# A last token tile computed in three column pieces, and a table of shifts in the order in which an attention and feed-forward kernel is recorded

## The chip, the cores and the metric

The kernel runs on one core of one Trainium2 chip. The core has a matrix engine (TensorE, PE in the profile, with its weight loads as PEld), a vector engine (VectorE, DVE), a scalar engine (ScalarE, ACT), a general engine (GpSimd, POOL) and a synchronisation engine (SyncE, SP), whose queue issues nearly all DMAs here. Every engine executes its own list of instructions in order; semaphores tie the lists together. The metric is the device time of one execution in microseconds.

## The reference

The input x has 2,048 tokens of 640 features. Two rounds run over it, with the same weights; each adds an attention with a memory and then a feed-forward network to x. In code cut to what matters:

```
x = x + A(layernorm(x))      # attention with memory
x = x + B(layernorm(x))      # relu(x @ w1) @ w2, 640 -> 1728 -> 640
x = x + A(layernorm(x))
x = x + B(layernorm(x))

A: q, k, v = x @ wq, x @ wk, x @ wv; 32 heads of 20; 4 segments of 512 tokens
   for each segment s:
     a_dot = softmax(q k^T / sqrt(20), causal inside the segment) v
     a_mem = phi(q) M / (phi(q) z)         # phi(t) = t + 1 if t > 0 else exp(t)
     o = g * a_mem + (1 - g) * a_dot       # g = sigmoid(beta), per head
     M, z = M + phi(k)^T v, z + sum(phi(k))
   return o @ wo
```

## The kernel before

All weights and all of x stay in the core's fast memory. Work is cut by round (0 or 1, called a or b) and segment (0 to 3, s), written (round, segment) below, and inside a segment by token tiles of 128 (four, NJ) and by groups of four heads (eight, G).

For one segment of attention: layer norm of four token tiles (`lnorm`, L705: statistics at L679 and L681, a small POOL power at L695, the normalised tokens at L725, then a transposing DMA issued by SP through `turn`, L701). Projections to q and k (`proj_part`, groups of five matmuls at L658 or L661, evacuated by ACT or DVE at L857/L858) and to v (`proj_v`, evacuated at L912). q and k go to a scratch tensor in HBM (`spill`, L946) and come back with four heads on separate partition groups (`fill`, L993, tile `pad`). Scores run as bursts of matmuls at L1177 into two PSUM slots, ACT takes their exponential (L1239) and POOL applies the causal mask (L1251). `apply` multiplies by v (L1271), `turn_pair` transposes the result back by DMA on SP (tile `otk` from `otu`), `divide` (L1357 to L1365) normalises it into `o_sb`, `mem_read` (L1057 to L1072) and `combine` (L1384) add the memory part, `turn_o` transposes `o_sb` on SP, and `out_proj` multiplies by wo and adds to x (L1393). Then the layer norm for the feed-forward network (`ln_b`), the network itself (`ffn` and `ffn_rest`, evacuated at L1475/L1476) and the addition to x through `add_half` (L1393). In round 1, `store` writes each token tile to the output (L1519).

A group of matmuls has two forms: whole (L658, 128 weight columns) and in quarters (L661, four matmuls of 32 weight columns that run beside each other). Scores use a third form, in which the rows are split. Whichever form is in force is kept where a group has both.

The order of all this is not written by hand. Each kind of work is a Python generator, a stream, that yields one step at a time: an operation, a need for an event, a slot of a buffer, or a spawned stream. `Sched.run` (L286) looks at the next step of every stream, works out from its own table of durations when the step could start, and records the step with the smallest key: start plus a lateness, then priority, then rank, then stream number (L319). Recording appends the step to its engine's list, and each engine on the chip then executes its list in that order. Whatever is recorded later sees the times and slots that the earlier choices left.

Streams are numbered in the order of `S.add` (L1541 to L1577), spawned ones after them:

```
 0 scores      1 exps        2 causal      3 apply       4 free_v
 5 turn_pair   6 divide      7 turn_o      8 out_proj(0) 9 out_proj(1)
10 ln_b(0)    11 ln_b(1)    12 fill       13 spill      14 combine
15 phi_(0)    16 phi_(1)    17 mem_read(0) 18 mem_read(1) 19 turn_k
20 mem_write  21 first_sums 22-25 first_one(0..3)       26 first_ln_b
27 proj_ln    28 proj_first 29 proj_one(0) 30 proj_one(1) 31 proj_v
32 ffn        33 ffn_rest   34 store      35 warm_pe    36 consts
37 loads      38 late_loads 39, 40, 41 ... spawned (the first ones by proj_first)
```

A stream made with `each` (L1525) goes through the eight (round, segment) pairs and has rank 4 x round + segment; the others have rank 0, and a spawned stream has the rank of its parent. `proj_ln` is the layer norm before attention, `ln_b(0)` and `ln_b(1)` are the first and the last two token tiles of the one before the feed-forward network.

For the second feed-forward product (L1502 to L1511) each of the four token tiles is made as two groups of 320 output columns, of 14 accumulating steps each; each group has a PSUM bank, and its addition to x is spawned as a stream. The store of a tile waits for both halves.

Of the kernel before, what the change touches and what calls it, by code (L numbers as in the profile page):

```python
# [7 lines left out]
ALU = mybir.AluOpType  # L8
# [5 lines left out]
NSEG = 4  # L14
# [5 lines left out]
NJ = L // 128  # L20
# [141 lines left out]
        self.gen = gen  # L162


LONE_NS = 300.0
SWITCH_NS = 96.0
COLS_LAG = 1500.0
# [9 lines left out]
class Sched:  # L177


    def __init__(self, prog):  # L180
        self.P = prog
        self.free = {e: 800.0 for e in ENGS}
        self.t = {}
        self.events = {}
        self.streams = []
        self.dma_free = 0.0
        self.rank = {}
        self.mode = "full"
        self.landed = set()

    def add(self, prio, gen):
        self.streams.append([prio, gen, None, None, False])
        self.rank[id(gen)] = 0

    def at(self, tk):
# [90 lines left out]
    def run(self):  # L286
        while True:
            best = None
            moved = True
            while moved:  # L290
                moved = False
                for st in list(self.streams):
                    had, ended = st[2], st[4]
                    self._settle(st)
                    moved = moved or st[4] != ended
                    moved = moved or st[2] is not had
            heads = []
            for n, st in enumerate(self.streams):
                if st[4]:
                    continue  # L300
                if isinstance(st[2], Op):
                    heads.append((st[0], n, st, self._alts(st[2]), st[2], self._late(st[2])))
                elif isinstance(st[2], Either):
                    both, lone = st[2].fn()
                    if both is not None:
                        heads.append((st[0], n, st, self._alts(both), both, 0.0))
                    if lone is not None:
                        heads.append((8, n, st, self._alts(lone), lone, LONE_NS))
            for prio, n, st, alts, op, late in heads:
                ok = []  # L310
                for end, start, k, e in alts:
                    if not any(p2 < min(prio, HOLDERS) and st2 is not st
                               and any(e2 == e and s2 + HOLD_TOL[e] < end for _, s2, _, e2 in al2[:1])
                               for p2, _, st2, al2, _, _ in heads):
                        ok.append((end, start, k))
                if not ok:
                    continue
                end, start, k = min(ok)
                key = (round(start + late), 0.5 if op.urgent else prio, self.rank[id(st[1])], n)  # L319
                if best is None or key < best[0]:  # L320
                    best = (key, st, end, start, k, op)
            if best is None:
                stuck = [st for st in self.streams if not st[4]]
                if not stuck:
                    return
                raise RuntimeError("stuck: " + "; ".join(
                    str(getattr(st[2], "key", None) or [s.name for s in getattr(st[2], "slots", [])][:2]) for st in stuck))
            _, st, end, start, k, op = best
            e, hold, fns, tail = op.alts[k]
            if e == "pe":  # L330
                op.mode = self._mode(op)
                self.mode = op.mode
                if op.mode == "cols" and op.cols is not None:
                    fns = op.cols
            waits, slot = op.waits, None
            for s in op.take:
                s.free = False
            if op.acq is not None:
                slot = self._pick(op.acq)
                slot.free = False  # L340
                waits = waits + slot.tks
                fns = [(lambda eng, fn=fn, slot=slot: fn(eng, slot), mark) for fn, mark in fns]
            self.P.waits(e, waits)
            self.free[e] = end
            if op.dma is not None:
                tk = self.P.dma(e, fns[0][0], op.dma)
                self.landed.add((id(tk[0]), tk[1]))
                self.dma_free = max(self.dma_free, start + 300.0) + tail[1]
                self.t[(id(tk[0]), tk[1])] = max(self.dma_free, end) + tail[0]
                if tail[2]:  # L350
                    self.free[e] = max(end, self.dma_free)
                out = tk
            else:
                marks = []
                for fn, mark in fns:
                    tk = self.P.op(e, fn, mark)
                    if tk is not None:
                        self.t[(id(tk[0]), tk[1])] = end + tail
                        marks.append(tk)
                out = marks[0] if len(marks) == 1 else (marks or None)  # L360
            st[2], st[3] = None, ((slot, out) if slot is not None else out,)
# [52 lines left out]
def bass_interleave_layers__memory_aug_infini_attn__dense_activation_relu__prompt_kernel(  # L414
    nc, A_x, A_wq, A_wk, A_wv, A_wo, A_beta, B_x, B_w1, B_w2, out,
):
    with contextlib.ExitStack() as es:
# [3 lines left out]
        S = Sched(P)  # L421
# [21 lines left out]
        x_sb = sb("x_sb", [128, TT, D])  # L443
# [25 lines left out]
        MISC = [Slot(ps[:, 4 + k, :], "misc%d" % k) for k in range(4)]  # L469
# [922 lines left out]
        def add_half(t, hf, bk, tk, waits=()):  # L1392
            ta = yield dve(320, 1, lambda e: e.tensor_tensor(  # L1393
                x_sb[:, t, 320 * hf:320 * hf + 320], x_sb[:, t, 320 * hf:320 * hf + 320], bk.ap[:, 0:320], ALU.add),
                [tk] + list(waits), urgent=True)
            bk.release(ta)
            return ta
# [67 lines left out]
        def ffn(b, s):  # L1465
            xtk = yield Need("hx", b, s)
            xt, xtk = xtk[0], xtk[1:]
            yield Acq([HT])
            S.set("hT", b, s)
            w1t = yield Need("w10")  # L1470
            hr = [("hr", b, s, dc) for dc in range(NFULL)]
            tk = None

            def square(dc, bk, tk):
                th = yield evac(512, 1, lambda e: e.tensor_scalar(hT[:, dc, :], bk.ap[:, :], 0.0, None, ALU.max),  # L1475
                                lambda e: e.activation(hT[:, dc, :], bk.ap[:, :], ACT.Relu), [tk] + HT.tks)  # L1476
                bk.release(th)
                S.set("hr", b, s, dc, tks=[th])

            for dc in range(NFULL):  # L1480
                if dc >= 2:
                    yield Need(*hr[dc - 2])
                if 128 * (dc + 1) > DFF // 2 >= 128 * dc:
                    w1t = yield Need("w11")
                bk, tk = yield from group(MISC, L, [
                    (w1_r[:, k, dc * 128:(dc + 1) * 128], feat(xt, k)) for k in range(FC)], xtk + w1t)
                yield Spawn(6, square(dc, bk, tk))
            HALF[b, s, 0] = tk
            if (b, s) in HALF:
                xt.release(tk, HALF[b, s])  # L1490
            w2t = yield Need("w2")
            hrest = yield Need("hR", b, s)
            sums = [[] for _ in range(NJ)]

            def residual(i, hf, bk, tk):
                ta = yield from add_half(4 * s + i, hf, bk, tk)
                S.set("sum", b, s, 2 * i + hf)
                sums[i].append(ta)
                if len(sums[i]) == 2:
                    S.set("xB", b, s, i, tks=sums[i])  # L1500

            for i in range(NJ):  # L1502
                for hf in range(2):
                    cs = slice(hf * 320, (hf + 1) * 320)
                    if 2 * i + hf >= 2:
                        yield Need("sum", b, s, 2 * i + hf - 2)
                    bk, tk = yield from group(MISC, 320, [
                        (hT[:, dc, i * 128:(i + 1) * 128], w2_r[:, dc, cs], Need(*hr[dc])) for dc in range(NFULL)] + [
                        (hR[:, (i % 2) * 128:(i % 2) * 128 + 128], w2_r[:, NFULL + i // 2, cs], hrest)], w2t)
                    yield Spawn(6, residual(i, hf, bk, tk))  # L1510
            HT.release(tk)  # L1511

        def store(b, s):
            if b == 0:
                return
            for i in range(NJ):
                t = 4 * s + i
                tks = yield Need("xB", b, s, i)
                S.last = yield dma("sp", dout, 163840, lambda e, t=t: e.dma_start(  # L1519
                    out[0, t * 128:(t + 1) * 128, :], x_sb[:, t, :]), tks)  # L1520
# [90 lines left out]
```

## Time and profile before

| | us |
|---|---|
| median of 4 executions | 558.92 (557.24 to 560.11) |
| the profiled execution, its own time | 559.04 |
| its span, first to last instruction | 557.3 |
| PE busy | 546.0 |
| DVE busy | 415.6 |
| ACT busy | 405.6 |
| POOL busy | 191.6 |
| last matmul ends | 554.53 |

How to read it: busy is the time in which an engine executed an instruction, and matmuls overlap each other in a pipeline, so PE can be busy without being at its peak. Lines of a timeline give start, duration, engine, source line, operation, what is written and read, shape and count; in square brackets stands the idle time of the engine before it and what ended it. A list of waits gives engine, line and tile that waited, what it waited for, the total, the number of times and the longest. In a table of stretches each engine has its busy time and, in brackets, its instructions; PEclk is the granted clock of the matrix engine as a share of full speed, and the last two columns are the DMA engines' busy share and rate. SPq is SP's queue, which issues DMAs.

### The profile page before, as it was taken

Reading aid. Unit: us, or ns where it says so; the run is one execution under the profiler, and the core shown is the slowest. Engines: PE = TensorE matmul, PEld = TensorE weight load, DVE = VectorE, ACT = ScalarE, POOL = GpSimd, SP = SyncE. Lnnn points to the kernel's source line nnn. Section 1 sums busy time; section 2 is a strip of 40 time slices with the busy share of each in tenths; the row PEclk is TensorE's granted clock in tenths of the full one; section 3 lists DMA queues with packets and bytes.
Section 4 is the critical chain, followed back from the end, with each engine's and each line's share of the span. In section 5 each row is a group of like instructions: output and inputs, shape, how many; then the busy total and the mean of one; then the engine's idle time right before and its main releaser. Section 6 shows DMA issues by size and latency. Waiting matters only on the chain.

```text
span 557.3 us, 18813 instructions
## 1 busy us (share of the span) xinstructions
PE 546.0 (98%) x8209; PEld 307.5 (55%) x8209; DVE 415.6 (75%) x1062; ACT 405.6 (73%) x514; POOL 191.6 (34%) x302
## 2 busy tenths in 40 slices
PE   8998999999999999999999999999999999999998
PEld 7554554456454555646456554565555654666756
DVE  5967889888898898897778988889965767335102
ACT  5699889899667887797788887887765787432140
POOL 5346345333443344343433443335410433201000
PEclk9999999999999999999999999999999999999999
DMA  8696999844574158274284423772426512344101
GB/s 271 145 226 159 216 193 218 226 61 91 101 159 85 27 105 180 50 111 83 58 196 91 91 45 112 154 125 21 67 59 167 106 45 30 86 88 60 41 2 49
DMA packets 130003, 61.30 MB, mean 110 GB/s; under 512 B 108802, under 2 KB 119810, under 8 KB 129922
## 3 DMA queue, kind: packets, MB, share of 16 engines
q1 hardware_dynamic: 129504, 59.62, 49.7%
q8 instruction: 64, 1.05, 0.8%
q10 hardware_dynamic: 418, 0.49, 0.3%
q14 instruction: 17, 0.14, 0.1%
HBM read 20.57 MB, written 12.85 MB: 60 GB/s over the span
## 4 chain that ended last, share of the span: by engine, by line
PE 81%; DVE 7%; DMA 7%; ACT 2%; SPq 1%; issue 1%; POOL 0%; ACTq 0%; POOLq 0%
PE ps L658 38%; PE ps L661 24%; PE ps L1177 8%; PE ps L1271 6%; DMA otk<-otu 3%; ACT PT L1239 2%; PE ps L1057 1%; DMA pad<-scr 1%; PE ps L1114 1%; PE ps L635 1%; DMA xnT<-xn_tok 1%; PE ps L1451 1%; DMA phk<-phs 1%; DVE o_sb L1365 1%; PE ps L1310 1%; DVE xn_tok L725 1%
## 5 line engine op out<-in xcount | busy, mean ns | idle before, releaser
L1239 ACT ACTIVATE PT<-ps 128x1024 bf16<-128x1024 f32 x320 | 309.1, 1027 | 65.9 <-PE ps L1177 61.6
L1251 POOL TENSOR_SCALAR_AFFINE_SELECT PT<-PT 128x512 bf16<-128x512 bf16 x256 | 165.9, 666 | 267.7 <-ACT PT L1239 267.6
L1393 DVE TENSOR_TENSOR x_sb<-x_sb,ps 128x320 bf16<-128x320 bf16 x128 | 60.5, 479 | 69.2 <-PE ps L661 55.5
L658 PE MATMUL ps<-w_r,hT 128*128 128x320 bf16 x508 | 81.5, 300 | 0.0
L661 PE MATMUL ps<-xnT,w_r 128*32 128x512 bf16 x1144 | 68.3, 379 | 0.0
L1177 PE MATMUL ps<-pad 20*128 20x512 bf16 (+3 forms) x1024 | 63.4, 301 | 3.1 <-ACT PT L1239 2.0
L658 PEld LDWEIGHTS ps<-w_r,hT 128*128 128x128 bf16 x508 | 47.4, 98 | 23.7 <-issue 5.2
L658 PE MATMUL ps<-xnT,w_r 128*128 128x512 bf16 x234 | 57.7, 380 | 0.7 <-DMA xnT<-xn_tok 0.7
L679 DVE BATCH_NORM_STATS2 stats<-x_sb 128x6 f32<-128x320 bf16 x124 | 55.6, 471 | 3.1 <-DMA x_sb<-in_A_x_dram 2.7
L1476 ACT ACTIVATE hT<-ps 128x512 bf16<-128x512 f32 x57 | 34.1, 599 | 22.7 <-PE ps L661 20.8
L661 PE MATMUL ps<-w_r,hT 128*32 128x320 bf16 x1296 | 49.6, 299 | 0.0
L1177 PEld LDWEIGHTS ps<-pad 20*128 20x128 bf16 x1024 | 17.9, 92 | 54.8 <-issue 24.6
L1281 DVE CAST otu<-ps 128x512 bf16<-128x512 f32 x51 | 34.9, 684 | 11.6 <-PE ps L1271 11.4
L661 PEld LDWEIGHTS ps<-xnT,w_r 128*32 128x32 bf16 x1144 | 29.5, 97 | 24.3
L1271 PE MATMUL ps<-PT,v_aug 128*21 128x128 bf16 (+3 forms) x896 | 40.5, 301 | 0.0
L661 PEld LDWEIGHTS ps<-w_r,hT 128*32 128x32 bf16 x1296 | 34.2, 97 | 9.2
L1475 DVE TENSOR_SCALAR hT<-ps 128x512 bf16<-128x512 f32 x47 | 32.2, 685 | 6.8 <-PE ps L658 5.3
L658 PE MATMUL ps<-wo_r,oT 128*128 128x320 bf16 x223 | 35.4, 300 | 0.4 <-DVE x_sb L1393 0.4
L695 POOL TENSOR_TENSOR rstd<-lnU,mhalf 128x2 f32<-128x2 f32 (+2 forms) x26 | 20.6, 791 | 44.3 <-DVE lnU L691 42.1
L658 PEld LDWEIGHTS ps<-xnT,w_r 128*128 128x128 bf16 x234 | 20.9, 97 | 24.5 <-issue 5.3
L1022 ACT ACTIVATE stg<-stg 128x512 bf16<-128x512 bf16 x50 | 31.5, 634 | 2.5 <-DVE rtmp L1020 2.2
L857 DVE CAST stg<-ps 128x512 bf16<-128x512 f32 x43 | 29.2, 683 | 5.2 <-PE ps L658 4.8
(108 smaller groups left out, 707.9 us busy)
## 6 DMA issues: line engine op xcount, KB each, us to landing
pad<-scr SPq DMA_DIRECT2D x124, 80.0 KB
scr<-stg SPq DMA_DIRECT2D x34, 256.0 KB, 3.3
out_dram<-x_sb SPq DMA_DIRECT2D x16, 160.0 KB, 1.8
w_r<-in_B_w_dram SPq DMA_DIRECT2D x10, 216.0 KB, 2.6
w_r<-in_B_w_dram SPq DMA_DIRECT2D x13, 160.0 KB, 2.9
x_sb<-in_A_x_dram SPq DMA_DIRECT2D x10, 160.0 KB, 3.3
scr<-w_r SPq DMA_DIRECT2D x5, 256.0 KB, 2.7
wv_r<-in_A_wv_dram SPq DMA_DIRECT2D x1, 800.0 KB, 8.9
```

The lines of the kernel that those rows point to most:

```text
L658: return e.matmul(view(dst.ap, b), a, b, start=(k == 0), stop=(k == last))
L661: return e.matmul(view(dst.ap[rows], b), part, b, start=(k == 0), stop=(k == last))
L679: tk = yield dve(320, 1, lambda e, c2=c2: e.bn_stats(stats6[:, t % 12, c2, :], x_sb[:, t, c2 * 320:(c2 + 1) * 320]), xt)
L1022: te = yield act(512, lambda e, q=q: e.activation(q, q, ACT.Exp), [tr] + p, psum=False)
L1177: fns.append([(lambda e, z=z, j=j, hh=hh, N=N, o=o, sl=sl, q=hh % 2: e.matmul(slot.ap[:, q, o:o + N], sl.ap[32 * hh:32 * hh + DH, z, 0, 12 ...
L1239: tx = yield act(1024, lambda e, dst=dst, src=src: e.activation(dst, src, ACT.Exp, scale=SCALE), sc + pw)
L1251: tm = yield pool(600.0, lambda e, reg=reg: e.affine_select(out=reg, in_=reg, pattern=[[0, 4], [1, 128]], compare_op=ALU.is_ge, fill=0.0, ...
L1271: fns.append((lambda e, OD, j=j, hh=hh: e.matmul(OD.ap[32 * hh:32 * hh + DH + 1, 128 * j:L], VAUG[vx(a, s)][:, j, 4 * g + hh, :], pt.ap[:, ...
L1281: te = yield evac(L, 1, lambda e: e.tensor_copy(dst, OD.ap), lambda e: e.activation(dst, OD.ap, ACT.Copy), [tk] + OTU[0].tks)
L1393: ta = yield dve(320, 1, lambda e: e.tensor_tensor(x_sb[:, t, 320 * hf:320 * hf + 320], x_sb[:, t, 320 * hf:320 * hf + 320], bk.ap[:, 0:32 ...
L1475: th = yield evac(512, 1, lambda e: e.tensor_scalar(hT[:, dc, :], bk.ap[:, :], 0.0, None, ALU.max), lambda e: e.activation(hT[:, dc, :], b ...
L1476: lambda e: e.activation(hT[:, dc, :], bk.ap[:, :], ACT.Relu), [tk] + HT.tks)
```

## The change

It has three parts. In the last token tile of the last segment of round 1, the second group of 320 columns is made as two groups of 160, each with its own addition to x; the store of that tile becomes three stores of 320, 160 and 160 columns, each after its own addition. A table NUDGE, with thirteen entries (stream number, rank), adds a number of nanoseconds to the first part of the key of that stream's steps while it has that rank; it shifts the place in the order, not the start that the planner reckons with. And streams that have ended are dropped from the planner's list, with the stream number now kept in the stream itself, so that numbers stay the same.

```diff
--- before.py
+++ after.py
@@ -162,6 +162,21 @@
         self.gen = gen
 
 
+NUDGE = {
+    (5, 0): -100,
+    (8, 2): -100,
+    (11, 0): -900,
+    (14, 0): 200,
+    (18, 0): 900,
+    (24, 2): 200,
+    (27, 3): 100,
+    (27, 6): 450,
+    (34, 3): -450,
+    (35, 3): 200,
+    (38, 4): 450,
+    (39, 4): 450,
+    (41, 0): 450,
+}
 LONE_NS = 300.0
 SWITCH_NS = 96.0
 COLS_LAG = 1500.0
@@ -183,13 +198,15 @@
         self.t = {}
         self.events = {}
         self.streams = []
+        self.count = 0
         self.dma_free = 0.0
         self.rank = {}
         self.mode = "full"
         self.landed = set()
 
     def add(self, prio, gen):
-        self.streams.append([prio, gen, None, None, False])
+        self.streams.append([prio, gen, None, None, False, self.count])
+        self.count += 1
         self.rank[id(gen)] = 0
 
     def at(self, tk):
@@ -286,6 +303,7 @@
     def run(self):
         while True:
             best = None
+            self.streams = [st for st in self.streams if not st[4]]
             moved = True
             while moved:
                 moved = False
@@ -295,7 +313,8 @@
                     moved = moved or st[4] != ended
                     moved = moved or st[2] is not had
             heads = []
-            for n, st in enumerate(self.streams):
+            for st in self.streams:
+                n = st[5]
                 if st[4]:
                     continue
                 if isinstance(st[2], Op):
@@ -316,7 +335,7 @@
                 if not ok:
                     continue
                 end, start, k = min(ok)
-                key = (round(start + late), 0.5 if op.urgent else prio, self.rank[id(st[1])], n)
+                key = (round(start + late + NUDGE.get((n, self.rank[id(st[1])]), 0)), 0.5 if op.urgent else prio, self.rank[id(st[1])], n)
                 if best is None or key < best[0]:
                     best = (key, st, end, start, k, op)
             if best is None:
@@ -1492,22 +1511,26 @@
             hrest = yield Need("hR", b, s)
             sums = [[] for _ in range(NJ)]
 
-            def residual(i, hf, bk, tk):
-                ta = yield from add_half(4 * s + i, hf, bk, tk)
-                S.set("sum", b, s, 2 * i + hf)
+            def residual(i, hf, bk, tk, c0, n):
+                t = 4 * s + i
+                ta = yield dve(n, 1, lambda e: e.tensor_tensor(
+                    x_sb[:, t, c0:c0 + n], x_sb[:, t, c0:c0 + n], bk.ap[:, 0:n], ALU.add), [tk], urgent=True)
+                bk.release(ta)
+                S.set("sum", b, s, 2 * i + hf, tks=[ta])
                 sums[i].append(ta)
                 if len(sums[i]) == 2:
                     S.set("xB", b, s, i, tks=sums[i])
 
             for i in range(NJ):
-                for hf in range(2):
-                    cs = slice(hf * 320, (hf + 1) * 320)
+                last = (b, s, i) == (1, NSEG - 1, NJ - 1)
+                for hf, c0, n in ((0, 0, 320), (1, 320, 160), (2, 480, 160)) if last else ((0, 0, 320), (1, 320, 320)):
+                    cs = slice(c0, c0 + n)
                     if 2 * i + hf >= 2:
                         yield Need("sum", b, s, 2 * i + hf - 2)
-                    bk, tk = yield from group(MISC, 320, [
+                    bk, tk = yield from group(MISC, n, [
                         (hT[:, dc, i * 128:(i + 1) * 128], w2_r[:, dc, cs], Need(*hr[dc])) for dc in range(NFULL)] + [
                         (hR[:, (i % 2) * 128:(i % 2) * 128 + 128], w2_r[:, NFULL + i // 2, cs], hrest)], w2t)
-                    yield Spawn(6, residual(i, hf, bk, tk))
+                    yield Spawn(6, residual(i, hf, bk, tk, c0, n))
             HT.release(tk)
 
         def store(b, s):
@@ -1515,6 +1538,12 @@
                 return
             for i in range(NJ):
                 t = 4 * s + i
+                if (s, i) == (NSEG - 1, NJ - 1):
+                    for hf, c0, n in ((0, 0, 320), (1, 320, 160), (2, 480, 160)):
+                        tks = yield Need("sum", b, s, 2 * i + hf)
+                        S.last = yield dma("sp", dout, 256 * n, lambda e, c0=c0, n=n: e.dma_start(
+                            out[0, t * 128:(t + 1) * 128, c0:c0 + n], x_sb[:, t, c0:c0 + n]), tks)
+                    return
                 tks = yield Need("xB", b, s, i)
                 S.last = yield dma("sp", dout, 163840, lambda e, t=t: e.dma_start(
                     out[0, t * 128:(t + 1) * 128, :], x_sb[:, t, :]), tks)
```

## The prediction

> **What bounds the kernel now.** I read the busy table of the page first, then the busy time by stretch, then what the matmul engine waited for, and last the timeline of the end.
>
> ```profile
> PE 546.0 (98%) x8209; PEld 307.5 (55%) x8209; DVE 415.6 (75%) x1062; ACT 405.6 (73%) x514; POOL 191.6 (34%) x302
> PE 81%; DVE 7%; DMA 7%; ACT 2%; SPq 1%; issue 1%; POOL 0%; ACTq 0%; POOLq 0%
> ```
>
> PE is busy for 98% of the span and carries 81% of the chain that ended last. Next, eight stretches; the first two numbers are the length and PE's busy time in it.
>
> ```profile
> 0.00:20.00 20.00, 17.74 (x156) 13.65 (x157) 12.82 (x38) 10.12 (x23) 7.34 (x23) 1.00 0.67 204
> 20.00:110.00 90.00, 87.36 (x1189) 45.24 (x1190) 75.95 (x208) 82.15 (x104) 40.18 (x61) 1.00 0.88 209
> 110.00:160.00 50.00, 49.42 (x631) 27.50 (x623) 43.68 (x108) 41.46 (x51) 19.34 (x30) 1.00 0.51 100
> 160.00:240.00 80.00, 78.68 (x1092) 41.80 (x1094) 70.49 (x186) 63.49 (x75) 32.07 (x49) 1.00 0.44 91
> 240.00:350.00 110.00, 109.96 (x1490) 58.27 (x1490) 91.45 (x222) 91.52 (x113) 46.31 (x69) 1.00 0.49 101
> 350.00:430.00 80.00, 78.29 (x1205) 43.68 (x1194) 63.66 (x162) 59.71 (x79) 24.11 (x36) 1.00 0.50 96
> 430.00:484.00 54.00, 54.00 (x720) 30.28 (x719) 37.35 (x93) 40.22 (x46) 20.72 (x33) 1.00 0.35 73
> ```
>
> PE's idle time, length less busy, is 2.64 + 0.58 + 1.32 + 0.04 + 1.71 + 0.00 = 6.29 us from 20 to 484 us. That is nearly all a better order can win: the work itself is not changed, and from 484 us on PE has only feed-forward matmuls left and runs through to 554.5. The granted clock is 1.00 throughout. A burst of scores (L1177) between other matmuls also costs a change of array form, which this table counts as busy: in the records a gap of about 108 ns lies on either side of a burst. The number of bursts stays; two bursts placed together would save two gaps, 0.2 us. What PE waited for:
>
> ```profile
> PE ps L1177 <- ACT PT L1239: 2.0, 4, 0.7
> PE ps L635 <- POOL mhalf L585: 1.6, 1, 1.6
> PE ps L1177 <- DMA pad<-scr: 1.0, 2, 0.8
> PE ps L658 <- DVE w_r L857: 0.9, 1, 0.9
> PE ps L658 <- DMA xnT<-xn_tok: 0.7, 1, 0.7
> ```
>
> Each is a single case of at most 0.9 us (the 1.6 is the start): places where the recorded order reached something that came late. There is no one large stall to remove.
>
> **The last tile.** The end of the timeline, and the store line's landing:
>
> ```profile
> 552.32 0.31 PE L661 MATMUL ps<-w_r,hR 128*32 128x320 bf16 x4
> 552.46 1.94 PE L661 MATMUL ps<-w_r,hT 128*32 128x320 bf16 x52
> 554.22 0.31 PE L661 MATMUL ps<-w_r,hR 128*32 128x320 bf16 x4
> 554.58 0.49 DVE L1393 TENSOR_TENSOR x_sb<-x_sb,ps 128x320 bf16<-128x320 bf16 x1 [1.42 <-PE ps L661]
> ...
> DMA to landing us min/median/max: 1.8/1.8/4.1
> ...
> 395.91 0.34 PE L1057 MATMUL ps<-BD,phs 128*32 128x147 bf16 x12
> 396.09 1.04 PE L661 MATMUL ps<-xnT,w_r 128*32 128x512 bf16 x16
> ```
>
> After the last matmul (554.53) come a 0.49 us add, the issue at 555.10, 1.79 us to landing and 0.4 us to the end.
>
> PE: a 320-column group takes 554.22 - 552.32 = 1.90 us for 56 quarter matmuls. Its second half becomes two groups of 160. The nearest narrow row is memory reading in the same form: 12 matmuls of 147 columns start within 396.09 - 395.91 = 0.18 us, 15 ns each, so 56 of 160 take 56 x 15 x 160/147 = 0.92 us, and two groups 1.84 to 1.90 us. I take +0.0. From the other side, a matmul of 160 columns that took as long as one of 320 would make the extra group cost a full 1.90 us; the 147 row is so near that I keep only +0.3 as the bad end.
>
> A rule speaks against the halving here. "TensorE: Matmul & The Clock Gate", section "LDWEIGHTS (loading the stationary operand)", has a load cost its columns divided by 1.2 in ns, whatever the rows; 32 columns are then 27 ns, and by it, as an estimate, two groups of 56 loads would take 3.0 us instead of 1.90, which would turn this part into a loss of 1.1 us. The row with a load and a matmul every 15 ns contradicts that for quarter loads.
>
> DVE: the last add falls from 320 to 160 columns. An add of 128x320 takes 489 ns there; a two-input operation on 128x160 (L626) takes 316 ns. That is -0.17 us on the path. The extra add (316 ns) lies beside PE's last group.
>
> SP and DMA: one store becomes three. The first two leave beside the remaining matmuls, the second about 0.9 us before the third, and an issue holds SP for 0.33 us, so the third finds SP free. Of the 1.79 us from issue to landing, the packets take 0.61 us (128 of 1,280 bytes, 55 ns each, by the DMA records); 256-byte packets take 18 ns and 512-byte ones 27, so 320-byte ones should take about 21 and the burst 0.25 us: -0.3 us, at best -0.5, and at worst +0.2 if writes this short cost extra. Together: 0.0 - 0.17 - 0.3 = **-0.47 us**, between -0.7 and +0.5.
>
> **The table.** Keys are (stream number, rank). Streams are numbered in the order of the S.add calls, and only those made by `each` or spawned from one carry a rank above 0. So (24,2), a first_one, (35,3) warm_pe, (38,4) late_loads and (39,4), the first spawned, never have that rank; (14,0) combine and (18,0) mem_read issue nothing in segment 0; (34,3) store returns at once for b = 0. Seven entries of thirteen do nothing. The six others:
>
> - (41,0), +450: evacuation of the third projection group, on ACT at 10.80 us. ACT had been idle 1.14 us before it and no other work stands on ACT or PE in these microseconds, so recording it later changes no queue: 0.0, at worst 0.45 us, which is its whole shift.
> - (27,3), +100, and (27,6), +450: layer norm before attention for segments (0,3) and (1,2). Each is 17 DVE instructions, one POOL power and two SP transposes, of which DVE has 8 statistics at 471 ns and 4 normalisations at 521 ns. They let other DVE work by. The tokens are wanted some 100 and 40 us later (scores of (0,3) start near 181 us, of (1,2) near 351), so nothing behind waits. What can pay is DVE's other work: PE waited 0.4 us in all between 57 and 92 us, and nothing between 286 and 312. Gain 0 to 0.4.
> - (11,0), -900: second half of the layer norm before feed-forward of segment (0,0): 9 DVE instructions, one POOL power (0.80 us), one transpose on SP. They now stand from 78.36 to 88 us with gaps filled by casts and memory work. Recorded up to 0.9 us early they wait at the head of DVE's queue: for the residual adds, and for the power before the normalisation. Queued behind are casts (683 ns each) that free PSUM banks for PE. DVE is busy 32.00 of 35 us there, so it has 3.0 us to give. In return feed-forward (first at 91.19 us) can start earlier and fill PE. Between -0.4, the stretch's waits, and +0.9, one hold that passes through; I take 0.
> - (8,2), -100: out projection, left half, of segment (0,2): 20 matmuls and 4 adds from 195.6 on. A ready matmul (135 ns) goes ahead of a burst of scores. The nearest wait is 0.6 us, of scores on exps at 195.30. Between -0.6 and +0.3 (two matmuls ahead of a burst, ACT waiting); I take -0.2.
> - (5,0), -100: all 28 otk transposes on SP, 1.2 to 1.5 us each on the queue. Mostly the steps that they overtake belong to other engines, so SP's order stays: 0, unless a pad fill falls behind one (below).
>
> The direct sum, with half of the 0.4 for the norms, is -0.2 - 0.2 = -0.4 us. Beyond it, any change of order changes the planner's later choices, and the waits listed are dealt anew. Their squares (0.6, 0.7 and 0.2 on exps, 0.8 and 0.2 on pads, 0.9, 0.7, 0.4 and smaller) sum to about 3.6, so one deal scatters by 1.9 us and two against each other by 2.7: an estimate that takes the waits as independent. It favours no side.
>
> **Sum.** The profiled execution took 559.04 us: span 557.3 and 1.7 around it, 0.1 above the median 558.92. 559.04 - 0.47 - 0.4 = 558.2, and 558.1 against the median.
>
> **Rivals.**
> 1. The table finds an order without most of the waits. For it: 2.64 of the 6.29 us lie between 20 and 110 us, where three of the moved steps are. Against: 240 to 350 us, where the largest late shift sits, has 0.04 us to win. With 2.4 to 5 us of the 6.29 gone: 559.0 - 0.5 - 3.5 = 555.
> 2. Slower: at the end of segment (1,2) a pad fill leaves later. SP's queue there, and the wait that it already causes:
>
> ```profile
> 415.34 1.42 SPq L946 DMA_DIRECT2D scr<-stg  x2
> 418.25 2.91 SPq L701 DMA_TRANSPOSE oT<-o_sb  x2
> 421.26 1.73 SPq L993 DMA_DIRECT2D pad<-scr  x4
> 423.04 1.32 SPq L946 DMA_DIRECT2D scr<-stg  x3
> ...
> 426.15 0.40 PE L1177 MATMUL ps<-pad 20*128 20x512 bf16 x4 [0.84 <-DMA pad<-scr]
> ```
>
> PE has used up its other work at 425.3 and idles 0.84 us until the pads land, so there is no margin: each microsecond that a step ahead on SP is late is one of PE. One more pair of transposes ahead (2.91), or a wait at SP's head like that of this fill for the scratch (3.3), gives 559.0 - 0.5 + 3.3 = 561.8. It decides from 2.8 us of delay on.
> 3. The live entries change nothing of weight, and only the last tile tells: 558.5.
>
> **How the numbers follow.** Half a percent, 2.8 us, is about what a measurement of this kernel can tell from no change. Small gain with the waits about as many as before: 0.34; nothing but the tile: 0.06; both are within it. Rival 1: 0.34; rival 2 and other new stalls: 0.26. The likeliest time is 558.1; its own range is 556.2 to 561.6. Reaching into rival 1 (to 554, which wants 5 us of waits gone; 1 in 12 below) and rival 2 (to 562.6; 1 in 9 above) makes 554.0 to 562.6.
>
> **What would show it.** The last add 128x160 at about 0.32 us, three store issues, the last landing near 1.5 us; 128x160 groups that end within 0.1 us of today's pace. PE's idle time from 20 to 484 us between 4 and 8.5 us. Layer norm steps of (0,0) earlier than 84 to 88 us. Wrong if a PE wait over 2 us appears, if the number of changes of array form moves by more than ten (1.1 us), or if the idle falls under 4 us.

## The result and the profile after

The changed kernel takes 557.52 us where the kernel before takes 559.21, both medians: a ratio of 0.9967, 95% interval 0.9958 to 0.9976, or by that ratio 1.85 us less. The forecast was 558.1 against 558.92, 0.8 us less, with a range of 554.0 to 562.6 and "within half a percent" as the likeliest outcome. The direction and that outcome came true; the size is a little over twice the forecast, and it came from the table, the tile adding nothing that the runs can tell. The profiled execution took 557.63 us, 0.1 above its median, with a span of 555.8.

The busy table and the chain of the changed kernel (its lines are 19 further down than before for most of the program; the last additions to x are at L1516, the stores at L1544 and L1548):

```profile
PE 545.4 (98%) x8259; PEld 307.4 (55%) x8259; DVE 416.5 (75%) x1067; ACT 404.0 (73%) x510; POOL 192.6 (35%) x302
PE 85%; DVE 7%; DMA 5%; SPq 1%; ACT 1%; issue 1%; POOL 0%
```

The bound is the same engine. The stretches, length and PE's busy time first:

```profile
20.00:110.00 90.00, 85.68 (x1121) 44.48 (x1119) 73.94 (x202) 81.60 (x104) 40.31 (x61) 1.00 0.90 203
110.00:160.00 50.00, 49.84 (x732) 27.55 (x731) 45.40 (x111) 41.14 (x50) 19.36 (x30) 1.00 0.52 112
160.00:240.00 80.00, 79.82 (x1104) 43.15 (x1106) 69.98 (x185) 63.11 (x73) 32.24 (x49) 1.00 0.44 89
240.00:350.00 110.00, 109.74 (x1416) 57.78 (x1417) 90.41 (x221) 88.77 (x112) 42.59 (x65) 1.00 0.49 96
350.00:430.00 80.00, 79.92 (x1230) 44.52 (x1229) 64.97 (x167) 62.84 (x81) 27.42 (x41) 1.00 0.53 102
```

PE's idle from 20 to 484 us is 4.32 + 0.16 + 0.18 + 0.26 + 0.08 + 0.00 = 5.00 us, 1.29 less than before. It fell by 2.97 us between 110 and 430 and rose by 1.68 before 110. The last matmul ends at 552.77 in place of 554.53. The largest waits of PE:

```profile
PE ps L677 <- DVE om_sb L1091: 1.3, 1, 1.3
PE ps L1196 <- DMA pad<-scr: 1.0, 1, 1.0
PE ps L677 <- DVE w_r L876: 0.9, 1, 0.9
PE ps L1196 <- ACT PT L1258: 0.8, 2, 0.6
```

The first is new: at 107.5 us a feed-forward group waits for a PSUM bank that memory reading frees through DVE (L1091). The waits for x_sb, for the DMA transposes of xnT and for two of the exponentials are gone; one profiled execution each can't say which of these are gone for good, since single waits move from execution to execution (last section).

The end of the changed kernel, and how its three stores (L1544) land:

```profile
551.56 0.24 PE L680 MATMUL ps<-w_r,hR 128*32 128x160 bf16 x4
551.63 1.07 PE L680 MATMUL ps<-w_r,hT 128*32 128x160 bf16 x52
552.53 0.24 PE L680 MATMUL ps<-w_r,hR 128*32 128x160 bf16 x4
552.83 0.32 DVE L1516 TENSOR_TENSOR x_sb<-x_sb,ps 128x160 bf16<-128x160 bf16 x1 [0.65 <-PE ps L680]
...
L1544 SPq DMA_DIRECT2D out_dram<-x_sb x3: 332/332/1055, 551.4 to 553.2; - x3
DMA to landing us min/median/max: 2.1/2.2/2.9
...
q8 instruction: 65, 1.06, 0.8%
```

A group of 160 columns takes 552.53 - 551.56 = 0.97 us and the add 0.32 us, as forecast. But the third issue holds SP for 1.055 us in place of 0.33, and the landings take 2.1 to 2.9 us where 1.5 was forecast. From the last matmul to the end are 3.04 us, against 2.76 before. The last line counts 16 KB packets of instructions: 65, before 64. The 65th runs from 552.46 to 553.86 us, while all three stores are in flight (issued at 551.40, 552.21 and 553.17, landed at 553.52, 555.12 and 555.40).

### The profile page after: what moved, and what is told of

Its sections match the earlier page's. It is cut to its first block, busy times and chain, and to the rows that moved or that the text cites. A ratio compares the mean times of both kernels' runs of the same rounds, so it can differ in the third digit from the quotient of the medians.

```text
span 555.8 us, 18919 instructions
## 1 busy us (share of the span) xinstructions
PE 545.4 (98%) x8259; PEld 307.4 (55%) x8259; DVE 416.5 (75%) x1067; ACT 404.0 (73%) x510; POOL 192.6 (35%) x302
## 3 DMA queue, kind: packets, MB, share of 16 engines
q8 instruction: 65, 1.06, 0.8%
## 4 chain that ended last, share of the span: by engine, by line
PE 85%; DVE 7%; DMA 5%; SPq 1%; ACT 1%; issue 1%; POOL 0%
PE ps L677 41%; PE ps L680 25%; PE ps L1196 8%; PE ps L1290 6%; DMA pad<-scr 1%; PE ps L1133 1%; PE ps L1329 1%; PE ps L1076 1%; DMA otk<-otu 1%; DMA oT<-o_sb 1%; PE ps L1470 1%; DVE stats L698 1%; DVE o_sb L1384 1%; DMA scr<-stg 1%; DVE v_aug L931 1%
## 5 line engine op out<-in xcount | busy, mean ns | idle before, releaser
L677 PE MATMUL ps<-w_r,hT 128*128 128x320 bf16 x467 | 75.1, 300 | 0.0
L1516 DVE TENSOR_TENSOR x_sb<-x_sb,ps 128x320 bf16<-128x320 bf16 (+1 forms) x65 | 31.1, 479 | 49.1 <-PE ps L680 39.0
L677 PE MATMUL ps<-xnT,w_r 128*128 128x512 bf16 x263 | 65.0, 380 | 1.3 <-DVE om_sb L1091 1.3
L680 PE MATMUL ps<-xnT,w_r 128*32 128x512 bf16 x1028 | 61.3, 379 | 0.0
L680 PE MATMUL ps<-w_r,hT 128*32 128x320 bf16 (+1 forms) x1512 | 56.1, 295 | 0.0
L677 PEld LDWEIGHTS ps<-w_r,hT 128*128 128x128 bf16 x467 | 43.7, 98 | 22.4 <-issue 5.9
L680 PEld LDWEIGHTS ps<-w_r,hT 128*32 128x32 bf16 x1512 | 38.7, 97 | 10.8 <-DVE x_sb L1412 0.2
L1412 DVE TENSOR_TENSOR x_sb<-x_sb,ps 128x320 bf16<-128x320 bf16 x64 | 29.8, 478 | 16.1 <-PE ps L680 9.1
L1494 DVE TENSOR_SCALAR hT<-ps 128x512 bf16<-128x512 f32 x51 | 34.8, 683 | 5.5 <-PE ps L677 4.5
L680 PEld LDWEIGHTS ps<-xnT,w_r 128*32 128x32 bf16 x1028 | 26.3, 97 | 21.8
```

The lines of the kernel that those rows point to most:

```text
L677: return e.matmul(view(dst.ap, b), a, b, start=(k == 0), stop=(k == last))
L680: return e.matmul(view(dst.ap[rows], b), part, b, start=(k == 0), stop=(k == last))
L1516: ta = yield dve(n, 1, lambda e: e.tensor_tensor(x_sb[:, t, c0:c0 + n], x_sb[:, t, c0:c0 + n], bk.ap[:, 0:n], ALU.add), [tk], urgent=True)
```

## Experiments

Theory T is the prediction's: a shorter tail (-0.47 us), and entries that cost or gain little by themselves and deal the waits anew. Against it stand F, in which an extra block of instructions collides with the stores, and for the table that an entry pushes a whole segment's scores back.

First a fact that needs no run. With (41,0) and the seven entries that never meet a step taken out, every engine's list of instructions and waits is that of the changed kernel; with (5,0) alone in the table it is that of the kernel before; with (27,3) alone it differs from it in the order of five instructions on DVE and in one wait of PE. So three entries are left to do the work: (11,0), (8,2) and (27,6). No run has (27,3) alone.

**The last tile alone (e1).**

```diff
 NUDGE = {
-    (5, 0): -100,
...
-    (41, 0): 450,
 }
```

> The last tile in three pieces, with an empty table: every engine's list is that of the kernel before up to the last token tile. Theory T, the prediction's: the add is 0.17 us shorter and the landing 0.3 us, so about -0.47 us, ratio 0.9991; the last landing 1.5 us after its issue. Rival F: the 56 extra matmuls and as many weight loads make one more block of PE's instructions, the 65th 16 KB packet on the instruction queue, which lands on the DMA engines beside the last stores as in the changed kernel (552.46 us, 1.40 us long); then the last issue takes near 1.05 us in place of 0.33, the last landing 2.2 us, and the end comes 3.0 us after the last matmul in place of 2.76: ratio 1.000 to 1.001.

Ratio 1.0011 (0.9991 to 1.0031): no gain that shows, though the interval still reaches T's 0.9991, so that the stores must decide. There are 65 blocks again; the 65th lands from 557.00 to 557.97 us in this execution, and SP's stores, the third issue again too long:

```profile
L1544 SPq DMA_DIRECT2D out_dram<-x_sb x3: 332/332/815, 555.7 to 557.5; - x3
DMA to landing us min/median/max: 1.7/2.0/2.5
```

The end comes 2.78 us after the last matmul: neither the 2.3 that T would give nor F's 3.0, and no better than the 2.76 of the kernel before.

**The table alone (e2).**

```diff
-                last = (b, s, i) == (1, NSEG - 1, NJ - 1)
+                last = False
```

and the store as before.

> The table with the last tile as before. Both theories of the tile: the whole of PE's saved waits is here. Prediction's sum for the table alone: -0.4 us and a deal of the waits with a scatter of 2.7 us; from the trace of the changed kernel, PE idle 1.3 us less between 20 and 484 us: ratio 0.997 (-1.7 us). If T holds for the tile, this run is 0.5 us slower than the changed kernel (0.9976); if F holds, it is 0 to 0.3 us faster (0.9965).

Ratio 0.9971 (0.9960 to 0.9982): all of the change's gain, with the tile adding nothing that shows beside it. It lies between the 0.9976 of T and the 0.9965 of F and decides nothing between them. PE's idle from 110 to 430 is 0.76 us here, 0.68 in the changed kernel.

**The last tile in the whole form (e3), and in two halves (e4).** In e3 the groups of the last tile have 14 matmuls of 128 weight columns in place of 56 of 32:

```diff
-        def group(slots, n, mms, waits):
+        def group(slots, n, mms, waits, whole=False):
+            either_ = (lambda op, cols: op) if whole else either
...
-                        (hR[:, (i % 2) * 128:(i % 2) * 128 + 128], w2_r[:, NFULL + i // 2, cs], hrest)], w2t)
+                        (hR[:, (i % 2) * 128:(i % 2) * 128 + 128], w2_r[:, NFULL + i // 2, cs], hrest)], w2t, last)
```

> Empty table, last tile in three pieces, but its matmuls in the whole form (14 matmuls a group in place of 56), which takes some 250 PE instructions out against e1. F: no 65th block is fetched, the last issue is 0.33 us and the last landing 1.5 us; time -0.47 us plus about 0.1 for one change of array form, ratio 0.9993, and the end 2.4 us after the last matmul. T, in which fetching has no part: the tail as in e1, +0.1 us against it.

Its stores:

```profile
L1544 SPq DMA_DIRECT2D out_dram<-x_sb x3: 332/332/332, 553.6 to 555.4; - x3
DMA to landing us min/median/max: 1.5/1.5/1.6
...
q8 instruction: 64, 1.05, 0.8%
```

64 blocks, no long issue, landings of 1.5 us: the end comes 2.3 us after the last matmul, 0.5 less than before. This is the forecast's tail, term by term, with the same 320-byte runs; so the runs' length was not what made them slow. The ratio, 0.9993 (0.9979 to 1.0007), agrees but cannot tell it from no change by itself. e4 keeps two groups of 320 and stores each by itself:

```diff
-                for hf, c0, n in ((0, 0, 320), (1, 320, 160), (2, 480, 160)) if last else ((0, 0, 320), (1, 320, 320)):
+                for hf, c0, n in ((0, 0, 320), (1, 320, 320)):
...
-                    for hf, c0, n in ((0, 0, 320), (1, 320, 160), (2, 480, 160)):
+                    for hf, c0, n in ((0, 0, 320), (1, 320, 320)):
```

> Empty table, last tile as two groups of 320 as before, each stored by itself (two stores of 640-byte runs in place of one of 1,280); no PE instruction is added. F: 64 blocks, issue 0.33 us, landing 1.6 us (packets of 640 bytes take about 33 ns, 8 on each DMA engine, against 58): -0.2 us, ratio 0.9997. If short runs themselves land late, the landing is 2.1 us or more, as the first store of the last tile in the changed kernel, and the time is 0.3 us longer: 1.0005.

Ratio 0.9995 (0.9981 to 1.0009), 64 blocks, the last landing 1.58 us. F is right about the tile.

That it is the overlap in time, and not the number 65, shows in other kernels: e8 below has 65 blocks, none at its very end, and its last store lands in 1.79 us. In e11 a plain store of 1,280-byte runs is issued at 554.50, a block lands from 554.96 to 556.29, and that store takes 3.0 us to land, where its neighbour without a block beside it takes 1.78. The single packets show which part is late. Of the 128 packets of the first of the three stores in the changed kernel 120 are through at 552.65, and the other 8 start from 553.84 on, as the block ends (553.86); of the store in e11 120 are through at 555.92, and the other 8 start from 556.28 on (block's end 556.29). Why the third issue holds SP longer was not followed.

The Trainium skill, "Runtime: NRT & Kernel Launch", section "Instruction fetch mechanics", says that an engine's instructions are refilled in blocks of 16 KiB by DMA and that crossing a block's boundary is mostly hidden. The size agrees with the packets here. Hidden it is from PE, but not from a store that is in flight beside the block.

**Each entry alone, and the pairs (e5 to e8, e10, e11).** The last tile is as before in all of them. e5, e6 and e7 have one entry each; e8, e10 and e11 are the table without (8,2), without (27,6) and without (11,0). In these pairs (5,0) and (27,3) stay in; they change nothing but the few DVE lines. The table of e5, and that of e8:

```diff
 NUDGE = {
+    (27, 6): 450,
 }
```

```diff
 NUDGE = {
+    (5, 0): -100,
+    (11, 0): -900,
+    (27, 3): 100,
+    (27, 6): 450,
 }
```

> The table holds (27, 6): 450 alone, the last tile as before. Prediction: the steps have 40 us to spare, so nothing waits behind them; 0 to -0.4 us, ratio 1.000. Rival: pushing this layer norm back makes the score chain of a later segment late, and PE runs out of other work before its pads land: an idle stretch of 2 to 5 us between 340 and 430 us, ratio 1.004 to 1.009; then the other entries of the table have to make up for it.

> The table holds (11, 0): -900 alone, the last tile as before. Prediction: 0 for the step itself (-0.4 to +0.9) and a new deal of all waits after 77 us. If the gain of the table is this entry's, PE's idle from 20 to 484 us is about 5.0 us and the ratio 0.997; if the gain comes only from the entries together, idle is 6 us or more and the ratio 0.999 to 1.004.

> The table holds (8, 2): -100 alone, the last tile as before. The lists are those of the kernel before up to about 196 us. Prediction: -0.2 us (-0.6 to +0.3) for the step, and a new deal of the waits after 196 us, of which the kernel before has 1.71 us of PE idle between 350 and 430. Ratio 0.998 if that idle goes, 1.000 to 1.003 if it stays or grows.

> The table without (8, 2), the last tile as before: what (11, 0) and (27, 6) do together. If the entries add up, this is e2 plus 0.2 us. If they work only in a set, each dealing the waits after it anew, the kernel is a different order from 196 us on and PE's idle between 240 and 430 us moves by 1 to 3 us either way: ratio 0.997 to 1.005.

> The table without (27, 6), the last tile as before. If (27, 6) is a plain loss of 4 us that the others hide, this kernel beats e2 clearly: ratio 0.993 or less. If entries only deal the waits anew, it lies anywhere in 0.995 to 1.003; layer norm of (1, 2) is not pushed back, so its scores start near 355 us and the last exponential ends near 480 to 487.

> The table without (11, 0), the last tile as before: (8, 2) and (27, 6). If (8, 2) is enough to keep the layer norm of (1, 2) in time, scores of (1, 2) start near 357 us as in the changed kernel and the ratio is 0.996 to 0.999. If it takes (11, 0) as well, they start near 385 us as in e5, PE runs out of work near 524 us, waits about 3 us for the last layer norm's transposes at a falling clock, and the ratio is 1.005 to 1.010.

| in the table | run | ratio (95%) | scores of (1,2) reach ACT | last exponential ends |
|---|---|---|---|---|
| nothing | before | 1 | 351.6 | 481.5 |
| (27,6) | e5 | 1.0090 (1.0071 to 1.0110) | 384.7 | 494.9 |
| (11,0) | e6 | 1.0024 (1.0004 to 1.0044) | 355.1 | 487.0 |
| (8,2) | e7 | 0.9963 (0.9947 to 0.9979) | 355.0 | 478.9 |
| (11,0), (27,6) | e8 | 0.9988 (0.9972 to 1.0004) | 381.2 | 491.2 |
| (8,2), (11,0) | e10 | 0.9986 (0.9972 to 0.9999) | 356.5 | 487.7 |
| (8,2), (27,6) | e11 | 1.0049 (1.0032 to 1.0066) | 384.1 | 494.2 |
| all | e2 | 0.9971 (0.9960 to 0.9982) | 357.0 | 481.8 |

Three things follow. The entries don't add up: alone they make +5.0, +1.3 and -2.1 us, +4.3 together if they added, and all three make -1.6. One entry of the thirteen, (8,2), does alone what all do (the intervals of e7 and e2 overlap), but beside either of the other two its gain is smaller or lost (e10, e11). And (27,6), which the prediction held to be harmless, is the most expensive: alone +0.9%, beside (8,2) still +0.5%. The rival named ahead of e5 had the price right (1.004 to 1.009) and the place wrong: PE has no idle stretch between 340 and 430 us. e11 came as the second of its two cases.

Where its time goes can be followed. The SP queue of the kernel before, from 308 us on, where the transposes of the layer norm of (1,2) are the pair from 313.29, and the stores of its q and k follow at 341:

```profile
313.29 9.57 SPq L701 DMA_TRANSPOSE xnT<-xn_tok  x2
341.34 4.42 SPq L946 DMA_DIRECT2D scr<-stg  x4
345.85 4.51 SPq L993 DMA_DIRECT2D pad<-scr  x12
```

And in e5, where by the order of recording the first pair belongs to the other layer norm, `ln_b` of segment (1,0), which has gone ahead, and the pair from 350.21 is that of (1,2):

```profile
336.83 2.88 SPq L720 DMA_TRANSPOSE xnT<-xn_tok  x2
350.21 3.01 SPq L720 DMA_TRANSPOSE xnT<-xn_tok  x2
373.98 3.56 SPq L965 DMA_DIRECT2D scr<-stg  x4
377.72 1.66 SPq L720 DMA_TRANSPOSE xnT<-xn_tok  x1
379.48 4.63 SPq L1012 DMA_DIRECT2D pad<-scr  x12
```

A shift of 0.45 us has become one of 37 us at the transposes and 33 at the scores. PE doesn't wait there: between 240 and 484 us it has work without a gap, since feed-forward fills in. The bill comes at the end, because what filled in is then missing. PE in e5:

```profile
523.97 0.31 PE L680 MATMUL ps<-w_r,hR 128*32 128x320 bf16 x4
527.23 1.26 PE L1470 MATMUL ps<-xnT,w_r 128*32 128x256 bf16 x20 [2.95 <-DMA xnT<-xn_tok]
528.25 3.09 PE L680 MATMUL ps<-xnT,w_r 128*32 128x512 bf16 x36
...
520.00:524.00 4.00, 4.00 (x128) 3.08 (x117) 2.58 (x8) 0.00 (x0) 0.70 (x1) 1.00 0.58 129
528.00:530.00 2.00, 2.00 (x32) 0.94 (x26) 0.00 (x0) 0.38 (x1) 0.00 (x0) 0.50 0.00 0
532.00:534.00 2.00, 2.00 (x44) 1.05 (x40) 0.00 (x0) 1.04 (x3) 0.00 (x0) 1.00 0.03 8
```

PE has nothing left at 524.3 and waits 2.95 us for the last layer norm's transposes. In the kernel before these land at 515.3, and PE has other matmuls until 524.57, a reserve of 9 us. After its wait PE runs at half clock in e5: by the clock records the granted share is 0.50 from 526.79 to 530.21, 3.41 us, of which PE works 2.98, a loss of 1.5 us. Wait and clock make 4.4 us in this execution; in all six of e5 the mean granted clock is 0.997 or lower. The entry costs 5.0, and the 1.4 us that lists without it wait between 350 and 430 are not there in e5, so about 2 us of its cost were not placed. e11 shows the same pair in its profiled execution, a wait of 2.93 us and a half clock from 525.75 for 3.41 us; but two of its six executions have a mean clock of 1.000 and take 561.56 and 561.87 us against a median of 561.71, so the clock's part does not show in its times. The Trainium skill, "TensorE: Matmul & The Clock Gate", section "What's actually happening", describes such windows of 3,413 ns and a clock of 4/8 after an idle one; length and level agree with the rows, though here a wait of 2.95 us, less than a window, was enough.

Late scores alone are not what costs. e8 has (27,6) too, beside (11,0), and its scores of (1,2) come 30 us late; but the last transposes land at 522.1, 5 us earlier than in e5, and PE just gets there. The kernel before, then e8:

```profile
524.57 0.72 PE L1451 MATMUL ps<-xnT,w_r 128*32 128x256 bf16 x20
...
522.23 0.73 PE L1470 MATMUL ps<-xnT,w_r 128*32 128x256 bf16 x20 [0.19 <-DMA xnT<-xn_tok]
```

e8 has used up the whole reserve and pays 0.19 us, with a ratio of 0.9988; e5 and e11 go about 3 us past it.

In e6, (11,0) alone, the waits are at other places: 1.7 us for the bank at 107.5 us, and the pads that the second rival named:

```profile
PE ps L677 <- DVE om_sb L1091: 1.7, 1, 1.7
PE ps L1196 <- DMA pad<-scr: 1.6, 2, 1.4
```

The wait for the bank near 107 us appears in every kernel with (11,0) (0.9 to 1.7 us) and in none without it. In e7, (8,2) alone, the lists are those of the kernel before up to about 196 us; PE's idle between 350 and 430 is gone:

```profile
160.00:240.00 80.00, 79.91 (x1109) 42.54 (x1106) 70.86 (x188) 63.13 (x74) 31.48 (x49) 1.00 0.42 92
240.00:350.00 110.00, 109.92 (x1445) 57.84 (x1441) 93.56 (x224) 92.72 (x114) 48.04 (x69) 1.00 0.48 94
350.00:430.00 80.00, 80.00 (x1193) 44.82 (x1186) 62.22 (x163) 60.88 (x79) 24.32 (x38) 1.00 0.56 112
```

It was 1.71 us before, and 1.29, 1.15 and 1.34 in e1, e3 and e4, whose lists are the same there; and it is 0.56 in e9, which has e7's list; so 0.8 to 1.4 of e7's 2.1 us are placed. (The kernel before, e1, e3 and e4 also have a wait of 0.4 to 1.3 us near 165 us, and e7 and e9 do not; but that lies ahead of the first difference of the lists, so it is no work of (8,2).) Which later choices of the planner, after (8,2), removed the waits between 350 and 430, and why beside (27,6) it takes both (8,2) and (11,0) to keep the layer norm of (1,2) in time, was not followed choice by choice and stays open.

**Two versions put together (e9, e12).** e9 is e7 with e3's last tile, e12 the changed kernel with it.

> (8, 2): -100 alone, with the last tile in three pieces in the whole form (e7 and e3 together). If the two add up: 0.9963 x 0.9993, ratio 0.9955, 0.6 us under e7 and 1 us under the changed kernel; 63 or 64 blocks of instructions, last landing 1.5 us. If a deal of the waits decides, e7's order is kept up to the tile, so nothing there changes: a ratio over 0.997 would speak for e7 having been lucky.

> The changed kernel with the last tile's matmuls in the whole form. If the 65th block of instructions is what took the tile's gain, it is gone here: last issue 0.33 us, last landing 1.5 us, the end 2.3 us after the last matmul in place of 3.0: 0.6 us under the changed kernel and 0.4 under e2, ratio 0.996 to 0.9965. If something else in the three stores is slow, the end stays 2.8 us or more after the last matmul and the ratio is 0.997 or more.

e9: 0.9949 (0.9934 to 0.9965), 3.0 us under the kernel before and the lowest ratio of all (0.9955 was expected if e7 and e3 add up, and the interval holds it). So e7's order shows its gain a second time. The last landing takes 1.50 us and there are 63 blocks. e12: 0.9956 (0.9942 to 0.9970), 64 blocks, and the end 2.29 us after the last matmul. Against the changed kernel that is -0.6 us, as worked out from the stores, though the two intervals overlap.

## Why the prediction came out as it did

- **PE bounds, and its idle is what an order can win.** Right: PE's idle went from 6.29 to 5.00 us, inside the 4 to 8.5 named; with the same list up to the last tile it is 4.3 and 4.2 in e2 and e12. The number of changes of array form, 334 by the records, is the same before and after. One reading was too short: after 484 us PE's list held not only feed-forward but also 16 matmuls of `apply` and 160 of the out projection (6.3 us); they made PE wait 0.5 us in e6 and nothing in the kernels before and after.
- **The last tile, -0.47 us.** The mechanism was right and the sum not: its terms for PE (+0.0; measured 1.94 us for two groups against 1.90) and the add (-0.17; 0.32 us) held. The rule of the Trainium skill that spoke against the halving ("TensorE: Matmul & The Clock Gate", section "LDWEIGHTS (loading the stationary operand)") would have had 27 ns a load; the group runs at 17 ns a load and matmul. The term that failed is the landing, -0.3 us: it came to +0.4 in the changed kernel, with the third issue 0.7 us longer, because 112 more PE instructions brought one more block of instructions onto the DMA engines under the stores. What a part adds in instructions was counted as time on PE alone. Without the block (e3) the tail is the 0.5 us shorter that was forecast.
- **(41,0), (5,0), the seven dead entries: nothing.** Right, by the lists.
- **(27,6), "40 us to spare, so nothing behind waits", 0 to -0.4 us.** Wrong by 5 us for the entry alone. Slack was counted at the end of the chain, and the delay as 0.45 us once. But the shift counts at each of the 17 DVE steps, against every other stream that wants DVE, and by the order of recording the other layer norm went through between them; 33 us were lost (how much at which step was not measured), and the time was paid 140 us later in the reserve of matmuls at the end. (11,0) beside it is enough to bring the ratio back to 0.9988 (e8), (8,2) is not (1.0049, e11).
- **(11,0), 0 us between -0.4 and +0.9.** Alone +1.3 us. The cost seen is of the kind named, DVE's queue freeing a bank late, but at memory reading at 107.5 us and not at the casts near 80.
- **(8,2), -0.2 us, -0.6 to +0.3 for the step.** Alone -2.1 us. The step itself cannot be seen; the gain came 150 us later.
- **"The waits are dealt anew, with a scatter of 2.7 us, no side favoured."** As a size this held: -2.1, +1.3, -0.7, -0.8 and -1.6 us lie within it, +2.7 for the pair of (8,2) and (27,6) at its edge, and only +5.0 for (27,6) alone is nearly twice as much. As a picture it fell short: waits were not dealt independently, one cause moved a whole segment. The forecast's -0.8 against -1.85 us is a deal somewhat better than the middle one, within the likeliest range of 556.2 to 561.6. That the sign came out is in part luck: of the 0.8 us forecast 0.47 were the tile's, which brought nothing (the end comes 3.04 us after the last matmul in place of 2.76), and the table's -0.4 came as about -1.6 by waits that the sum had not counted on.
- **The rivals.** The first, fewer waits, happened in part: 1.3 us of the 6.29 went. The second, pads late at the end of segment (1,2), did not happen in the changed kernel (0.0 us of PE idle from 430 on), but its wait shows in e6 and e10, 1.4 and 1.3 us near 430 us. The third, that only the tile tells, is refuted by e1 and e2: only the table did.

## What to carry to other kernels

In an order that a greedy planner makes, a small push on one stream need not be a small delay: it counts again at every step on a contested engine, and slack must be compared with the sum of what goes ahead, not with the push. Slack has to be followed to the end, too: a segment 30 us late cost nothing where the reserve of matmuls just lasted (e8) and 0.9% where it ran out (e5). Test each entry of such a table alone and against the set: here one of thirteen alone did as much as all, and another was a loss of 0.9% that the table had to cover. And when a long unrolled program grows by a few matmuls, look whether one more block of instructions comes in, and what it lands beside.

## What had not been expected of the hardware

Blocks of 16 KB of instructions, 63 to 65 of them, arrive all through the kernel, each in about 1 us, and a store in flight at that time can take 1 us longer to land (1.78 to 3.0 us) and hold its issuer's queue (0.33 to 1.06 us). Not every one does: in the kernel before a store issued at 551.29, 0.3 us ahead of a block's end, lands in 1.77 us.

A 3.41 us window at half clock also appears in some executions of one and the same list: in e3 and e5, whose lists are those of the kernel before so far, it lies at 55.6 and 55.8 us, behind a PE wait of 0.9 us near 54.5, and not in the other profiled executions, though each of them has that wait. Of 54 executions of the changed kernel the 7 with a mean granted clock below 0.9985 have a median of 558.97 us and the other 47 one of 557.42. So 1.5 us of difference between two single executions can go with the clock.

Waits move from execution to execution under the same list: PE's idle from 20 to 110 us is 2.64, 4.39, 2.59, 2.32, 3.08 and 3.66 us in six kernels (before, e1, e3, e4, e7, e9) whose lists agree to 196 us. The rise of 1.68 us there in the changed kernel is partly such scatter; the wait for the bank, 1.3 us, is not.
